# Block sums of the w_k gradient placed in other memory, and the sums at the start of the last stage put in another order

## The chip, the cores and the metric

One core of one Trainium2 chip runs the whole program in one launch. The metric is device time in microseconds (us), the median of several runs; lower is better. TensorE is called PE here, VectorE DVE, ScalarE ACT, GpSimd POOL, and SP is the queue from which most transfers are issued.

## The reference

The kernel computes one transformer block and all its gradients for one sequence of S = 2048 rows, D = 640, F = 1728, 32 heads of 20, all bf16:

```python
h  = x + A(layernorm(x))          # A: linear attention with wqkv, wo
h2 = h + B(layernorm(h))          # B: (silu(x @ w_gate) * (x @ w_up)) @ w_down
out, vjp = jax.vjp(f, A_x, A_wqkv, A_wo, B_w_gate, B_w_up, B_w_down)
return (out, *vjp(grad_out))
```

Three results matter for the change. `out_1` is the gradient of x; its last step is a layer norm backward over `dxn`, the gradient of the normalised input. `out_2` holds the gradient of wqkv; its middle third, the w_k gradient, is `xn.T @ dk`, a sum over 2048 rows. `out_0` is `h + m @ w_down`, where m is the product of the two gates.

## The kernel before

**Stages.** The program goes through the forward pass, the gate and up products with their gradients, and the attention gradients. Its last two stages are those that the change touches. The first is a loop (L1050 on) over t = 0 to 18. In step t it makes tile t of `dk` (128 rows; PE, then DVE L1057 to L1063), transposes it by DMA into the buffer `ring`, and for tile u = t - 3 makes `ps_dxn` on PE (L1095, 30 matmuls), and then the layer norm backward `ln_bwd` (L141 to L152): ACT scales the row (`lb_dy`, L144), DVE multiplies and sums (L146), scales two sums (L149), ACT makes `lb_a` (L150), DVE adds twice (L151, L152) into `dx`, and POOL issues the store of `dx` to `out_1` (L1103). In steps 16 to 18 there is no `dk` tile left, only `dxn` tiles 13, 14 and 15.

**The last stage** (from L1222) makes the w_k gradient and then `out_0`. Both are 2 x 2 block products in Winograd's form, which takes seven products in place of eight for the price of sums of blocks; DVE makes the sums with `tt` (L1033).

- For the w_k gradient the halves of the 2048 rows and the two halves of 640 columns are the blocks. Sums of blocks of xn are S1, S2, S3 (two of each, u = 0 and 1, 128 x 1024), sums of blocks of dk are X1 to X4 (128 x 2560, tile `dt`). S1 and S3 lie in the tile `sk`, and are made inside the loop above, at steps 16 to 18 (`ksum`). PE's products are `ps_ka` and `ps_kc` (L1162, by `prod`). The first products, of plain blocks, need no sum. The next, `ps_kc`, needs S1 and X1. Four small products `dwo` (L1110) stand between them. The last 128 rows of the gradient are outside the 2 x 2 scheme, and are made plainly, in three pieces of 320, 192 and 128 columns by `k_tile` (L1341) at the very end.
- For `out_0`, eight pairs p of row tiles go through `step_a` to `step_f` (PE: `ps_oa`, `ps_oc`). Sums of w_down's blocks are T1 to T5 (tile `ot`, T3 in place in `wd`), made once. Sums of m's blocks are four for each pair (`osum(p, 0)` to `osum(p, 3)`, in the tile `os`), of transposed tiles of m (`mT`, loaded by DMA, L1028). `step_d` and `step_e` of pair p - 1 stand between the steps of pair p.

**What sets the order.** PE, ACT, DVE and SP run in the order written here (`manual_schedule`); each engine does its instructions one after the other, and an instruction that waits holds up all those behind it. POOL's order is found by the framework. Work tiles come from pools with a fixed number of buffers; a new tile takes the place of an older one, and its first writer waits until all readers of that one are done, a store by DMA included. Four buffers of the pool `strips` and five of `big` are the places for the large tiles; four banks of PSUM are shared by all products (`mm`). The tiles of `ln_bwd` (`lb_dy`, `lb_a`, `dx`) come from a pool of six; before, all three of a row tile are taken together.

**Where the tiles lie before.** `mT` number 0 takes the place of the first `dq` tile, and `sk` that of the second, which SP still reads for the last transpose `ring<-dq` (L973). S2 lies in `os`; `os` has the place of `dh1`, which the last `dx` reads, and `dt` that of `wqkvT`, which the last `dxn` reads.

Of the kernel before, what the change touches and what calls it, by code (L numbers as in the profile page):

```python
# [20 lines left out]
def kernel(  # L21
# [40 lines left out]
    def mm(name):  # L62

        return psum.tile([P, 2, 512], FP32, name=name, tag="mm")
# [73 lines left out]
        eng.tensor_scalar(out=v[:, :nt], in0=mv[:, :nt, 1], scalar1=1e-5, scalar2=None, op0=ALU.add)  # L138
        nc.gpsimd.tensor_tensor(out=rstd[:, t0:t0 + nt], in0=v[:, :nt], in1=nhalf[:, :nt], op=ALU.pow)

    def ln_bwd(ps, xhat, rstd_col, resid, dst, pool):  # L141
        sums = small.tile([P, 2], FP32, name="lb_s", tag="lb_s")
        dy = wk("lb_dy", pool=pool)
        nc.scalar.activation(out=half(dy[:]), in_=row(ps), func=ACT.Copy, scale=rstd_col, accum_out=sums[:, 0:1])  # L144
        a = wk("lb_a", pool=pool)
        nc.vector.tensor_tensor_reduce(out=a[:], in0=dy[:], in1=xhat, scale=1.0, scalar=0.0,  # L146
                                       op0=ALU.mult, op1=ALU.add, accum_out=sums[:, 1:2])
        k = small.tile([P, 2], FP32, name="lb_k", tag="lb_k")
        nc.vector.tensor_scalar(out=k[:], in0=sums[:], scalar1=-1.0 / D, scalar2=None, op0=ALU.mult)  # L149
        nc.scalar.activation(out=a[:], in_=xhat, func=ACT.Identity, scale=k[:, 1:2], bias=k[:, 0:1])  # L150
        nc.vector.tensor_tensor(out=a[:], in0=a[:], in1=dy[:], op=ALU.add)  # L151
        nc.vector.tensor_tensor(out=dst, in0=a[:], in1=resid, op=ALU.add)  # L152

# [769 lines left out]
    with tc.manual_schedule(engines={EngineType.SP, EngineType.DVE}):  # L923
# [119 lines left out]
        def ksum(i, u):  # L1043

            if i == 1:
                tt(sk_v(1, u), xb(1, 0, u), xb(1, 1, u), ALU.add)
            else:
                tt(sk_v(3, u), xb(0, 0, u), xb(1, 0, u))

        for t in range(ST + LAG):  # L1050
            if t in (2, 3):
                dwqk(0, t + 1)
            if t < ST:
                if t + 2 < ST:
                    load_pk(t + 2)
                pkr = pkrs.pop(t)
                nc.vector.tensor_scalar(out=pkr[:], in0=pkr[:], scalar1=-1e-6, scalar2=1.0, op0=ALU.add, op1=ALU.min)  # L1057
                tk = wk("tk", pool=1)
                ps = mm("ps_dk")
                mm_row(ps, lambda i: xnT_r[:, t, i, :], lambda i, n0, n1: WK2[:, i, n0:n1], DT)  # L1060
                nc.vector.scalar_tensor_tensor(out=half(tk[:]), in0=row(ps), scalar=rstd1[:, t:t + 1] if t < NC else 1.0,
                                               in1=half(dzb[:]), op0=ALU.mult, op1=ALU.add)
                nc.vector.tensor_tensor(out=dk[:, t, :], in0=tk[:], in1=pkr[:], op=ALU.mult)  # L1063
                nc.sync.dma_start_transpose(out=ring[:, t % 4], in_=dk[:, t, :])
                if t < 2:
                    load_pqT(t + 1)
            if 8 <= t < 8 + HG:
                tr_cols(G[:, t - 8, :], scr_GT, OH[t - 8])
            if t == 14:
                nc.sync.dma_start_transpose(out=KV.rearrange("p j c -> p (j c)").unsqueeze(1), in_=scr_KVT)  # L1070
            if t == ST:
                dKV = stage()[:, :HG, :]
                nc.sync.dma_start_transpose(out=dKV, in_=dKVT.rearrange("p j c -> p (j c)"))
            if t == ST:
                wd = big.tile([P, FT, D], BF16, name="wd", tag="B")
                nc.sync.dma_start(out=wd[:, :13, :], in_=B_w_down[0:13 * P, :].rearrange("(j p) d -> p j d", p=P))
                for r in (0, 64):
                    nc.sync.dma_start(out=wd[r:r + 64, 13, :], in_=B_w_down[13 * P:F, :])
            u = t - LAG
            if u < 0:  # L1080
                continue
            if t == ST:
                sk = strips.tile([P, 7 * 8 * P], BF16, name="sk", tag="S")
                ksum(1, 0)
            if t == ST + 1:
                ksum(3, 0)
                ksum(3, 1)
            if t == ST + 2:
                ksum(1, 1)
            pkT, dqT, dkT = ring[:, 4 + u % 3], ring[:, 7 + u % 3], ring[:, u % 4]  # L1090
            ps = mm("ps_dxn")
            for ci, (n0, n1) in enumerate(NCH):
                for k, (lhs, rhs) in enumerate(((dqT, wqkvT[:, 0:5]), (pkT, WV2), (dkT, wqkvT[:, 5:10]))):
                    for i in range(DT):
                        nc.tensor.matmul(ps[:, ci, :320], lhsT=lhs[:, i, :], rhs=rhs[:, i, n0:n1],  # L1095
                                         start=(k == 0 and i == 0), stop=(k == 2 and i == DT - 1))
            if u + 3 < ST:
                load_pqT(u + 3)
            if ST - 4 <= u:
                load_mT(u - ST + 4)  # L1100
            dx = wk("dx")
            ln_bwd(ps, xn_r[:, u, :], rstd1[:, u:u + 1], dh1[:, u, :], dx[:], 0)
            nc.gpsimd.dma_start(out=o1_v[:, u, :], in_=dx[:])  # L1103

        def dwo(j):
            h0, h1 = HC[j]
# [19 lines left out]

        NP = ST // 2
        HK = 6
        os = big.tile([P, ST * D], BF16, name="os", tag="B")
        dt = big.tile([P, 4, 8, 320], BF16, name="dt", tag="B")  # L1130
        ot = strips.tile([P, 3 * HK * 320 + D], BF16, name="ot", tag="S")
        B11, B12 = wd[:, 0:HK, 0:320], wd[:, 0:HK, 320:D]
# [1 line left out]
        T1, T2, T4 = (ot[:, i * HK * 320:(i + 1) * HK * 320].rearrange("p (k n) -> p k n", k=HK) for i in range(3))  # L1134
        T3 = B12
        T5 = ot[:, 3 * HK * 320:3 * HK * 320 + D].rearrange("p (k n) -> p k n", k=2)
        f32 = os[:, 8 * HK * P:].bitcast(FP32)
        s1h, u3h, *u2h = (f32[:, 320 * i:320 * i + 320] for i in range(4))

        def os_v(p, i):  # L1140
            o = (4 * (p % 2) + i) * HK * P
            return os[:, o:o + HK * P].rearrange("p (k c) -> p k c", c=P)
# [81 lines left out]
        with tc.manual_schedule(engines={EngineType.PE, EngineType.Activation}):  # L1224
# [1 line left out]
            K21, K22 = dk[:, 8:16, 0:320], dk[:, 8:16, 320:D]  # L1226
            X1, X2, X3, X4 = (dt[:, i] for i in range(4))
            S1, S3 = [sk_v(1, u) for u in U], [sk_v(3, u) for u in U]
            S2 = [os[:, (3 + u) * 8 * P:(4 + u) * 8 * P].rearrange("p (k c) -> p k c", c=P) for u in U]
            kept = sk[:, 4 * 8 * P:4 * 8 * P + 4 * D].bitcast(FP32).rearrange("p (k u n) -> p k u n", k=2, u=2)  # L1230

            def k_store(ev, m, n):
# [4 lines left out]

            for t in range(4):
                load_h1(t)
            for t in range(4, 7):  # L1240
                load_mT(t)
            for j in range(2):
                tr_cols(Y[:, j, :], scr_Yt, OH[j])
            pk_a = [mm("ps_ka") for _ in U]
            for u in U:
                prod(pk_a[u][:, 0, :320], xb(0, 0, u), K11, True, 8)
            tt(X1, K12, K11)
            for u in U:
                prod(pk_a[u][:, 1, :320], xb(0, 1, u), K21, True, 8)
            for u in U:  # L1250
                tt(S2[u], S1[u], xb(0, 0, u))
            tt(X2, K22, X1)
            ev = wk("dwk", pool=1)
            for u in U:
                s1 = wk("s1", pool=u).bitcast(FP32)
                nc.scalar.copy(out=s1, in_=pk_a[u][:, 0, :320])
                tt(ev[:, 320 * u:320 * u + 320], pk_a[u][:, 1, :320], s1, ALU.add)
            k_store(ev, 0, 0)
            dwo(0)
            pk_c = mm("ps_kc")  # L1260
            for u in U:
# [10 lines left out]
            for u in U:  # L1272
                prod(pk_a[u][:, 0, :320], S3[u], X3, False, 8)
                nc.scalar.copy(out=kept[:, 1, u, :], in_=pk_a[u][:, 0, :320])
            for u in U:
                tt(S1[u], xb(0, 1, u), S2[u])
            dwo(3)
            ev = wk("dwk", pool=0)
            tt(half(ev[:]), pk_c[:, :, :320], kept[:, 1], ALU.add)
            k_store(ev, 1, 1)  # L1280
            tt(T2, B22, T1)
            osum(0, 1)
            ev = wk("dwk", pool=1)
            for u in U:
                prod(pk_a[u][:, 0, :320], xb(1, 1, u), X4, False, 8)
                nc.scalar.copy(out=ev[:, 320 * u:320 * u + 320], in_=pk_a[u][:, 0, :320])
            k_store(ev, 1, 0)

            def k_last(u):
                prod(pk_c[:, u, :320], S1[u], K22, False, 8)  # L1290

            for p in range(NP):
# [8 lines left out]
                    tr_cols(Y[:, j, :], scr_Yt, OH[j])  # L1301
                step_a(p)
                if v < 0:
                    tt(T4, B21, T2)
                    tt(T3, B22, B12)
                    osum(p, 2)
                    k_last(0)
                    pcc = mm("ps_oc")
                    step_b(p)
                    k_last(1)  # L1310
                    ev = wk("dwk", pool=0)
                    tt(half(ev[:]), pk_c[:, :, :320], kept[:, 0], ALU.add)
                    k_store(ev, 0, 1)
                    step_c(p)
                    tt(T5, BL[0], BL[1])
                    osum(p, 3)
                    for i in range(4):
                        osum(p + 1, i)
                    continue
                step_d(v)  # L1320
                step_b(p)
# [9 lines left out]
                f(i)  # L1331

            v = NP - 1
            i = DT - 1
            ev = wk("dwk", pool=1)
            pk_l = mm("ps_kl")
            last = [(pk_l[:, 0, :320], 0, 320), (pk_l[:, 1, :192], 320, 512)]

            def k_tile(out, n0, n1, queue):
                for t in range(ST):  # L1340
                    nc.tensor.matmul(out, lhsT=xn_r[:, t, i * P:(i + 1) * P], rhs=dk[:, t, n0:n1],  # L1341
                                     start=(t == 0), stop=(t == ST - 1))
                nc.scalar.copy(out=ev[:, n0:n1], in_=out)
                queue.dma_start(out=out_2[i * P:(i + 1) * P, D + n0:D + n1], in_=ev[:, n0:n1])

            k_tile(*last[0], nc.sync)
            step_d(v)
            k_tile(*last[1], nc.sync)
            c22(v)
            step_e(v)  # L1350
            step_f(v)
# [31 lines left out]
```

## Time and profile before

| | |
|---|---|
| median of 3 runs | 801.03 us (800.27 to 803.26) |
| the profiled execution, its own time | 801.46 us |
| its span, first to last instruction | 799.7 us |
| outside the span | 1.76 us |
| busy, share of the span | PE 99%, DVE 73%, ACT 36%, POOL 22% |
| PE waits from 660 us on | 4.0 us before `ps_kc`, 0.8 us before a `ps_oa` |
| last matmul starts its group | 795.3 us |

Times inside the execution are counted from the start of the span. Names before `<-` are what an instruction writes, names after it what it reads, and L1162 is line 1162 of the kernel before. In the chain of waits, a line is a start time, a length and the work that held up the end at that moment. In the list of waits, a line says who waited, for whom, how long in all, how often, and the longest. In the timeline, start and length come first, and the brackets at the end tell how long the engine was idle before it.

### The profile page before, as it was taken

To read this page: it belongs to the slowest core of one execution; us is meant where nothing else is said; L and a number is where in the kernel's file an instruction comes from. 1 tells how busy PE (TensorE), PEld (TensorE's weight loads), DVE (VectorE), ACT (ScalarE), POOL (GpSimd) and SP (SyncE) were. 2 spreads that over 40 slices of the span, in tenths; PEclk is the share of its full clock that TensorE was granted. 3 is DMA by queue.
4 is the path that set the end of the run, shared out by engine and by line. 5 is a ranking of instruction groups with operands and counts; after the bars stand their busy time and mean duration, and the time that the engine had idled before them with its cause. 6 is when DMAs were issued, how large, how long until landed. Compare 5 with 4: busy or idle time off the path is not lost.

```text
span 799.7 us, 13627 instructions
## 1 busy us (share of the span) xinstructions
PE 789.5 (99%) x5295; PEld 504.1 (63%) x5295; DVE 582.5 (73%) x1038; ACT 288.7 (36%) x420; POOL 174.0 (22%) x308
## 2 busy tenths in 40 slices
PE   9999999999999999999999999999999999979998
PEld 7776566555555555555666777777777777756665
DVE  7989988894496648844965169999896366658773
ACT  6963532760383146303821232232322233332001
POOL 4600047411201110012142011121401111214220
PEclk9999999999999999999999999999999999999999
DMA  9899999999979897991797567776599769999952
GB/s 258 168 242 309 186 233 248 276 217 230 195 178 223 211 181 196 224 233 59 169 256 193 210 171 197 180 206 166 146 236 188 141 142 180 173 262 264 224 168 75
DMA packets 286994, 160.11 MB, mean 200 GB/s; under 512 B 241629, under 2 KB 275806, under 8 KB 286929
## 3 DMA queue, kind: packets, MB, share of 16 engines
q1 hardware_dynamic: 269056, 99.74, 61.6%
q0 software_dynamic: 14976, 54.20, 21.7%
q10 hardware_dynamic: 2896, 5.31, 2.1%
q8 instruction: 41, 0.67, 0.4%
q14 instruction: 25, 0.20, 0.1%
HBM read 47.68 MB, written 53.66 MB: 127 GB/s over the span
## 4 chain that ended last, share of the span: by engine, by line
PE 88%; DVE 5%; DMA 5%; ACT 0%; POOL 0%; SPq 0%; issue 0%; DVEq 0%
PE ps_dhn L108 15%; PE ps_dw L806 8%; PE ps_dxn L1095 7%; PE ps_wa L646 7%; PE pg L731 6%; PE pu L736 6%; PE ps_dm L417 5%; PE ps_oa L1162 4%; PE ps_kq L305 4%; PE ps_wc L646 3%; PE ps_dwqk L986 3%; PE ps_gt L861 3%; PE ps_dk L108 3%; PE ps_dp L108 3%; PE ps_y L508 3%; PE ps_a L571 3%
## 5 line engine op out<-in xcount | busy, mean ns | idle before, releaser
L108 PE MATMUL ps_dhn<-wgT,cols 128*128 128x320 bf16 x864 | 119.5, 299 | 0.0
L108 PEld LDWEIGHTS <-cols 128*128 128x128 bf16 x864 | 84.5, 98 | 32.9
L736 PE MATMUL pu<-wgu,hnT 128*128 128x448 bf16 (+1 forms) x320 | 63.6, 346 | 0.0
L731 PE MATMUL pg<-wgu,hnT 128*128 128x448 bf16 (+1 forms) x320 | 63.6, 346 | 0.0
L806 PE MATMUL ps_dw<-m_s,dh 128*128 128x448 bf16 (+1 forms) x320 | 60.4, 346 | 0.0
L1095 PEld LDWEIGHTS <-ring 128*128 128x128 bf16 x480 | 46.8, 98 | 18.8 <-DMA ring<-dq 0.7
L146 DVE CUSTOM_DVE_ANT_0 lb_a<-lb_dy,hn 128x640 bf16<-128x640 bf16 x32 | 26.4, 825 | 42.9 <-ACT lb_dy L144 42.9
L1095 PE MATMUL ps_dxn<-wqkvT,ring 128*128 128x320 bf16 x320 | 51.2, 299 | 0.0
L806 PEld LDWEIGHTS <-dh 128*128 128x128 bf16 x320 | 31.3, 98 | 27.1
L736 PEld LDWEIGHTS <-hnT 128*128 128x128 bf16 x320 | 31.3, 98 | 27.1
L731 PEld LDWEIGHTS <-hnT 128*128 128x128 bf16 x320 | 31.3, 98 | 27.0
L417 PEld LDWEIGHTS <-dh2T 128*128 128x128 bf16 x320 | 31.0, 98 | 25.1
L417 PE MATMUL ps_dm<-wdT,dh2T 128*128 128x448 bf16 (+1 forms) x240 | 46.5, 344 | 0.0
L144 ACT ACTIVATE lb_dy<-ps_dhn,rstd 128x640 bf16<-128x640 f32 x16 | 12.7, 794 | 91.7 <-PE ps_dhn L108 91.7
L305 PE MATMUL ps_kq<-wqk,xnT 128*128 128x320 bf16 x320 | 44.8, 299 | 0.2 <-DMA xnT<-xn 0.2
L752 ACT ACTIVATE dd<-pg 128x896 bf16<-128x896 f32 (+1 forms) x32 | 28.5, 891 | 40.4 <-PE pg L731 38.0
L642 DVE TENSOR_TENSOR dd<-dd 128x3584 bf16<-128x3584 bf16 (+1 forms) x12 | 23.1, 1954 | 25.3 <-PE ps_wa L646 15.6
L150 ACT ACTIVATE lb_a<-hn,lb_k 128x640 bf16<-128x640 bf16 x32 | 29.4, 920 | 27.8 <-DVE lb_k L149 24.8
L305 PEld LDWEIGHTS <-xnT 128*128 128x128 bf16 x320 | 30.9, 98 | 12.7 <-DMA xnT<-xn 0.5
L646 PEld LDWEIGHTS <-S 128*128 128x128 bf16 x256 | 25.0, 98 | 22.1 <-DVE dd L642 0.6
L772 POOL DMA_DIRECT2D scr_m<-m_s x16 | 12.1, 756 | 122.6 <-DVE m_s L764 122.6
L885 POOL DMA_DIRECT2D pqr<-scr_pq x16 | 8.8, 548 | 112.6 <-PE ps_dp L108 112.6
(227 smaller groups left out, 1566.5 us busy)
## 6 DMA issues: line engine op xcount, KB each, us to landing
scr_dT<-stg SPq DMA_DIRECT2D x48, 224.0 KB, 2.7
cols<-scr_dT POOLq DMA_DIRECT2D x6, 1728.0 KB, 9.0
scr_m<-m_s POOLq DMA_DIRECT2D x12, 448.0 KB, 4.8
cols<-scr_dT ACTq DMA_DIRECT2D x2, 1728.0 KB, 11.4
scr_dT<-stg SPq DMA_DIRECT2D x16, 192.0 KB, 2.3
scr_pq<-pqa SPq DMA_DIRECT2D x4, 640.0 KB, 4.6
scr_xnT<-xnT SPq DMA_DIRECT2D x4, 640.0 KB, 5.2
scr_pk<-pk SPq DMA_DIRECT2D x4, 640.0 KB, 4.6
```

Source lines behind the costliest of these rows:

```text
L108: nc.tensor.matmul(ps[:, ci, :320], lhsT=lhs(k), rhs=rhs(k, *NCH[ci]), start=(start and k == 0), stop=(stop and k == n - 1))
L146: nc.vector.tensor_tensor_reduce(out=a[:], in0=dy[:], in1=xhat, scale=1.0, scalar=0.0, op0=ALU.mult, op1=ALU.add, accum_out=sums[:, 1:2])
L150: nc.scalar.activation(out=a[:], in_=xhat, func=ACT.Identity, scale=k[:, 1:2], bias=k[:, 0:1])
L305: nc.tensor.matmul(ps[:, ci, :320], lhsT=xnT[:, t, k, :], rhs=wqk[:, k, w0 + n0:w0 + n1], start=(k == 0), stop=(k == DT - 1))
L417: nc.tensor.matmul(ps[:, c, :w], lhsT=dh2T[:, kt, (t + c) * P:(t + c + 1) * P], rhs=wdT[:, kt, o:o + w], start=(kt == 0), stop=(kt == DT - 1))
L646: nc.tensor.matmul(out, lhsT=lhs[:, t, :], rhs=rhs[:, t, :], start=(first and t == 0), stop=(t == 7), skip_group_check=not first)
L731: nc.tensor.matmul(pg[:, c, :w], lhsT=hnT[:, kt, (t + c) * P:(t + c + 1) * P], rhs=wg[:, kt, 0:w], start=(kt == 0), stop=(kt == DT - 1))
L736: nc.tensor.matmul(pu[:, c, :w], lhsT=hnT[:, kt, (t + c) * P:(t + c + 1) * P], rhs=wg[:, kt, w:2 * w], start=(kt == 0), stop=(kt == DT - 1))
L752: sig = nc.scalar.activation(out=dg, in_=pg[:, :, :w], func=ACT.Sigmoid)
L806: nc.tensor.matmul(ps[:, c, :w], lhsT=lhs(t), rhs=rhs(t), start=(t == 0), stop=(t == ST - 1))
L1095: nc.tensor.matmul(ps[:, ci, :320], lhsT=lhs[:, i, :], rhs=rhs[:, i, n0:n1], start=(k == 0 and i == 0), stop=(k == 2 and i == DT - 1))
L1162: nc.tensor.matmul(out, lhsT=lhs[:, k, :], rhs=rhs[:, k, :], start=(start and k == 0), stop=(k == n - 1), skip_group_check=not start)
```

## The change

1. `sk` is taken at step 15, ahead of `mT` number 0, so it has the place of the first `dq` tile, and `mT` number 0 that of the second. The sums S1 are both made at step 16 and the sums S3 both at step 17. The loads of `mT` begin one step later: the first is issued after the load of w_down (`wd`).
2. `ln_bwd` becomes a generator `ln_bwd_parts`, which pauses after ACT's `lb_a`. For the last row tile (u = 15) its first part runs after the order for X1, and its second part (`dx_end`) after the first eviction of the w_k gradient; so its tiles `lb_dy` and `lb_a` are taken after the four `h1r` buffers.
3. X1 is made ahead of that layer norm. S2 lies in `ot`; `os` is taken after `dx_end`.
4. T4, T5 and the sums for the first pairs are put in another order; the update of S1 (`xb(0, 1, u) - S2`) is made after an eviction in place of before it.
5. The 320-column piece of `k_tile` moves from ahead of the last `step_d` to pair 0, after `step_c`; its store goes to POOL's queue in place of SP's, and its evicted tile (`k_ev`) is taken there and held to the end.

```diff
-    def ln_bwd(ps, xhat, rstd_col, resid, dst, pool):
+    def ln_bwd(*args):
+        for _ in ln_bwd_parts(*args):
+            pass
+
+    def ln_bwd_parts(ps, xhat, rstd_col, resid, dst, pool):
...
         nc.scalar.activation(out=a[:], in_=xhat, func=ACT.Identity, scale=k[:, 1:2], bias=k[:, 0:1])
+        yield
         nc.vector.tensor_tensor(out=a[:], in0=a[:], in1=dy[:], op=ALU.add)
         nc.vector.tensor_tensor(out=dst, in0=a[:], in1=resid, op=ALU.add)
...
-            if t == ST:
+            if t == ST - 1:
                 sk = strips.tile([P, 7 * 8 * P], BF16, name="sk", tag="S")
-                ksum(1, 0)
-            if t == ST + 1:
-                ksum(3, 0)
-                ksum(3, 1)
-            if t == ST + 2:
-                ksum(1, 1)
+            if t in (ST, ST + 1):
+                for n in U:
+                    ksum((1, 3)[t - ST], n)
...
-            if ST - 4 <= u:
-                load_mT(u - ST + 4)
+            if ST - 3 <= u:
+                load_mT(u - ST + 3)
             dx = wk("dx")
-            ln_bwd(ps, xn_r[:, u, :], rstd1[:, u:u + 1], dh1[:, u, :], dx[:], 0)
+            ln = ln_bwd_parts(ps, xn_r[:, u, :], rstd1[:, u:u + 1], dh1[:, u, :], dx[:], 0)
+            if u == ST - 1:
+                break
+            for _ in ln:
+                pass
             nc.gpsimd.dma_start(out=o1_v[:, u, :], in_=dx[:])
+
+        def dx_end():
+            for _ in ln:
+                pass
+            nc.gpsimd.dma_start(out=o1_v[:, ST - 1, :], in_=dx[:])
...
-            S2 = [os[:, (3 + u) * 8 * P:(4 + u) * 8 * P].rearrange("p (k c) -> p k c", c=P) for u in U]
+            S2 = [ot[:, 2 * HK * 320 + u * 8 * P:2 * HK * 320 + (u + 1) * 8 * P].rearrange("p (k c) -> p k c", c=P)
+                  for u in U]
...
-            for t in range(4, 7):
+            for t in range(3, 7):
                 load_mT(t)
...
             for u in U:
                 prod(pk_a[u][:, 0, :320], xb(0, 0, u), K11, True, 8)
+            for u in U:
+                prod(pk_a[u][:, 1, :320], xb(0, 1, u), K21, True, 8)
             tt(X1, K12, K11)
-            for u in U:
-                prod(pk_a[u][:, 1, :320], xb(0, 1, u), K21, True, 8)
+            next(ln)
             for u in U:
                 tt(S2[u], S1[u], xb(0, 0, u))
             tt(X2, K22, X1)
...
             k_store(ev, 0, 0)
+            dx_end()
+            os = big.tile([P, ST * D], BF16, name="os", tag="B")
...
-            for u in U:
-                tt(S1[u], xb(0, 1, u), S2[u])
-            dwo(3)
             ev = wk("dwk", pool=0)
             tt(half(ev[:]), pk_c[:, :, :320], kept[:, 1], ALU.add)
             k_store(ev, 1, 1)
+            dwo(3)
+            for u in U:
+                tt(S1[u], xb(0, 1, u), S2[u])
...
                 step_a(p)
                 if v < 0:
-                    tt(T4, B21, T2)
                     tt(T3, B22, B12)
...
                     step_c(p)
+                    tt(T4, B21, T2)
+                    k_tile(mm("ps_kl")[:, 0, :320], 0, 320, nc.gpsimd)
+                    osum(p + 1, 0)
+                    osum(p + 1, 1)
                     tt(T5, BL[0], BL[1])
                     osum(p, 3)
-                    for i in range(4):
-                        osum(p + 1, i)
+                    osum(p + 1, 2)
+                    osum(p + 1, 3)
                     continue
...
-            k_tile(*last[0], nc.sync)
             step_d(v)
-            k_tile(*last[1], nc.sync)
+            k_tile(mm("ps_kl")[:, 0, :192], 320, 512, nc.sync)
             c22(v)
```

## The prediction on record

> **What bounds the kernel now.** The page's first part comes first: PE is busy 99% of the span, so only time that PE stands still, or runs at a lower clock, can be won; the change takes no matmul away. Whether there is such time in the last two stages, the list of waits of 690 to 800 us tells.
>
> ```profile
> PE ps_kc L1162 <- DVE dt L1033: 4.0, 1, 4.0
> ...
> ACT s L1256 <- DMA out_dram<-dx: 2.2, 1, 2.2
> ...
> PE ps_oa L1162 <- DVE h1r L1033: 0.8, 1, 0.8
> ```
>
> PE waits twice. Why the first wait is there, the chain of waits shows, read from the top:
>
> ```profile
> 702.48 3.97 DMA ring<-dq
> 706.53 0.69 DVE sk L1033
> 707.22 0.74 DVE lb_a L146
> ...
> 717.83 1.50 DVE dt L1033
> 719.37 3.18 PE ps_kc L1162 x16
> 722.56 0.53 PE ps_dwo L1110 x2
> 723.09 2.75 PE ps_ka L1162 x16
> 725.84 0.27 PE ps_dwo L1110 x2
> 726.11 2.17 PE ps_ka L1162 x16
> ```
>
> DVE stands still from 702.2 to 706.5: `sk` lies where the last transpose still reads `dq`. Three layer norms queue up behind it, and X1 (`dt`) behind them. The same lines hold a second loss: sixteen matmuls take 3.18 and 2.75 us after the wait and 2.17 at 726; two take 0.53 and then 0.27. The windows confirm it, granted clock third from the end:
>
> ```profile
> 715.00:720.00 5.00, 0.98 (x8) 0.50 (x7) 3.91 (x8) 1.87 (x4) 1.76 (x4) 1.00 1.21 277
> 720.00:725.00 5.00, 5.00 (x27) 3.07 (x25) 5.00 (x6) 1.30 (x3) 2.17 (x4) 0.66 1.22 261
> 725.00:730.00 5.00, 5.00 (x39) 3.62 (x37) 4.48 (x7) 3.00 (x7) 1.44 (x3) 1.00 1.20 323
> ```
>
> The second wait (741.36) has DVE behind it too: from 733.7 to 741.2 it worked without a pause on sums.
>
> [...] 4.0 us idle, then 0.66 granted over 5 us. [...] POOL's store of `dx` took 2.4 us from issue to landing when issued at 702.49, and 6.9 at 710.46, while the 2 MB of `wd` moved (issued at 707.01, 9.8 to landing).
>
> **The change part by part.** Clock as before up to 702.1, where DVE ends the `dx` of u = 12.
>
> *Sums in earlier memory.* The first `dq` tile was read for the last time many steps ago, so DVE needn't wait. Pitches from DVE's timeline: a 1024-wide sum 0.60, a whole layer norm from L146 to the end of L152 2.95 (707.14 to 710.09, ACT's turn included), a 2560-wide sum 1.40. Then: S1 to 703.3; layer norm 13 to 706.3; S3 to 707.5; layer norm 14 to 710.4; X1 must wait for the last `dxn` matmul (its place was `wqkvT`'s), which ends at 710.6, so it is done at 712.1, against 719.3 before. PE needs it when `ps_ka` (to 714.92) and `dwo(0)` (0.27) are through, at 715.2: 3.1 to spare. The wait goes: 4.01. With it goes the half clock: (3.18 - 2.17) + (0.53 - 0.27) + (2.75 - 2.17) = 1.85.
>
> *Split layer norm, and its new wait.* Taken after the four `h1r` buffers, `lb_dy` of u = 15 no longer gets an old `lb_dy` but the buffer of `dx` 13, whose store must land before ACT may write. The page of before has this kind of wait: ACT's `s` above waited 2.2 us for a store of `dx`. Now `dx` 13 is done at 706.3, and POOL issues its store 0.3 later (710.17 to 710.46 before), at 706.6. `wd` is issued 1.6 earlier than before, as no `mT` load (1.58 of SP) is ahead of it: at 705.4. [...] I take the 6.9 us seen in that position: landing at 713.5. Lower end 2.4, landing at 709.0; upper end: it drains with `wd` as before's did (710.46 + 6.87 = 717.33), 1.6 earlier, at 715.7. Queued behind that wait are, on ACT, `lb_a`, the two `s` and the copy of `dwo(0)`; on DVE all after X1. What must be met: L146 starts 1.0 after the landing (`lb_dy` 0.9); then L146 to L149 1.0, S2 1.2, X2 1.4, evictions 0.8, the split layer norm's end 0.94, X3 1.4: X3 is there 7.8 after the landing. PE wants it after `ps_kc` 2.17, `dwo` 0.27, `ps_ka` 2.17 and `dwo` 0.27, at 715.2 + 4.9 = 720.1. So PE loses (landing - 712.3): 1.2 at 713.5, nothing at 709.0, 3.4 at 715.7. The other needs (S2 and X2 at 717.6, the bank of `ps_kc` at 715.2) are met later than that value allows, so they add nothing. The store of `dx` 14, which `dx` 15 needs, is queued with the same load, but is wanted only some 6 us after.
>
> *Other memory for S2 and `os`.* `ot` lies where `ring` lay, whose last transpose landed at 706.5; S2 comes at 713: nothing. `os` waits for the split layer norm's end, and its first use is the sum after T1, seven DVE steps later: nothing.
>
> *`mT` behind `wd`.* In sum the queue carries the same bytes. The second `mT` tile took 10.0 from 709.74, so it landed at 719.7; it keeps that place, and the first now comes shortly before it. DVE wants the second at 721.3 or later, PE the first at 724.7: nothing, with 1.6 of cover. Lost cover would cost PE its lateness one for one.
>
> *Order of T4, T5 and the sums.* T4 (1.07) and two sums pass each other, the amount is the same. DVE is now ahead of PE here, because `k_tile` (2.18) gives it time: from the end of `step_c` it has an eviction 0.5, T4, five sums and T5, 3.9, and two evictions 0.9, in all 5.5 with a step between engines; PE has 2.17 for `k_tile` and 4.05 (736.48 to 740.53 before) until `step_c` of pair 1, 6.2. So the wait of 0.84 goes, with 0.7 to spare.
>
> *Moved chunk.* The same 16 matmuls in another place: nothing on PE. At the end, `step_d` of the last pair now follows `dwv` at once. It needs the eviction of `step_c`, which DVE ended at 786.3, and `dwv` ended at 788.3: covered by 2.0. Its store is one POOL issue of 0.54 behind an ACT copy, ahead of an `h1r` load wanted 20 us later; SP loses one issue. `k_ev` holds one of seven buffers for the stage; loads of `h1r` led their use by over 10 us, and a buffer comes free each 7.25: covered.
>
> *Sum.* 4.01 + 1.85 + 0.84 - 1.2 = 5.5 us. The profiled execution, 801.46, would take 796.0 (span 799.7 to 794.2). The median of the runs is 0.43 below that execution; the gain taken off it: 801.03 - 5.5 = 795.5.
>
> **The rivals.**
>
> *A: the store isn't in the way.* `dx` 13 gets into the engines before `wd`, or between its packets. For it: `dx` 12 took 2.4 among transposes. Against: `wd` has a lead of 1.2 us. Gain 6.7: 794.3.
>
> *B: the store drains with `wd`.* For it: before's store landed at 717.3, just past `wd`'s 716.8. Against: it was issued late in that transfer, so the two ends had to be near. Loss 3.4, gain 3.3: 797.7.
>
> *C: slower than before, by the same wait.* If the store lands behind `wd` and the first `mT` load that now follows it, [...] the clock is halved again, 1.85. The change gains nothing once (landing - 712.3) + 1.85 exceeds 6.7, from a landing at 717.2 on; at 718.5 it is 6.2 + 1.85 = 8.1, a loss of 1.4: 802.4. For it: stores issued at 714.6, among `mT` loads, still took 4.4. Against: its own bytes are few, and `wd` starts earlier.
>
> *That the change does nothing* would need X1 to be late in another way; it has 3.1 us of cover, so I give it no chance of its own.
>
> **How the numbers follow.** Forecast 0.45, A 0.22, B 0.25, C 0.08. I predict 795.5; forecast and A together span 794.3 to 796.5 (a landing at 714.5). For 8 in 10 the range takes in A and B: down to 793.8 for 0.5 of scatter, up to 799.2, B with most of a half clock on top. About 0.5% (4.0 us) is what a measurement of this kernel can tell from no change. Faster by more than that, below 797.0: forecast, A and a little of B, 0.68. Within it: most of B, and C near its start, 0.28. Slower: 0.04.
>
> **What the profile would show.** Right: no wait of PE for `dt` and none for `h1r`; clock 1.00 from 715 to 730; DVE's `sk` straight after `dx` at 702; a wait of ACT's `lb_dy` for a store of `dx`, ending near 713.5; then a wait of PE of about 1 us in all before `ps_ka` or a `dwo`. Under A no such waits; under B about 3 us of them; under C a clock below 1. What would make it wrong: a landing other than that, or an `mT` tile later than 721.

## The result: 2 us of the 5.5 forecast

The changed kernel takes 799.18 us in the median of 20 runs (795.3 to 806.74), the kernel before 802.01 in 20 runs beside it (799.86 to 805.17): 0.9972 of the time before, 95% interval 0.9950 to 0.9994. The gain is about 2 us where 5.5 were forecast. In all, 56 runs of the changed kernel were made; their median is 800.0 us, against 801.97 in 221 runs of the kernel before. The profiled execution took 798.42 us, span 796.7; the last group of matmuls starts at 792.81 instead of 795.16 (by PE's timeline; the 795.3 in the table of before is the chain's reading of the same group).

The list of waits of the kernel after, 690 to 800 us (who waited, line, for whom; total, times, longest):

```profile
ACT lb_dy L148 <- DMA out_dram<-dx: 3.9, 1, 3.9
...
PE ps_dwo L1121 <- ACT dwo L1122: 2.1, 1, 2.1
...
PE ps_dwv L127 <- DMA mats<-scr_Yt: 1.7, 1, 1.7
...
PE ps_dxn L1097 <- DMA ring<-dq: 0.6, 1, 0.6
```

The waits of before for `dt` (4.0) and for `h1r` (0.8) are gone. Three others stand in their place, 4.4 us together against 4.85. The windows view (granted clock third from the end) says that in this execution the half clock went too:

```profile
715.00:720.00 5.00, 2.95 (x22) 1.99 (x21) 4.83 (x9) 2.25 (x4) 0.50 (x1) 1.00 1.00 168
720.00:725.00 5.00, 4.96 (x37) 3.59 (x37) 4.83 (x5) 2.56 (x5) 2.74 (x6) 1.00 1.13 266
```

The chain of waits of the kernel after (start, length, what held up the end):

```profile
704.95 11.13 DMA wd<-in_B_w_down_dram
...
719.29 0.70 ACT dwo L1122
719.99 0.04 issue
720.03 0.43 PE ps_dwo L1121 x2
720.47 2.17 PE ps_ka L1169 x16
...
753.60 5.31 DMA mats<-scr_Yt
758.91 0.05 issue
758.95 0.19 PE ps_dwv L127
```

Where before DVE's `sk`, `lb_a` and `dt` stood, the chain now runs through transfers: first `wd`, then the transposes of `Yt`, which `ps_dwv` reads. The first link needs care. The instruction behind it on DVE (S2) waits for several things, and the view names one; DVE's `lb_k` had ended at 715.97, just before S2 began at 716.11, so it was the late layer norm that held S2. (In `a3` below S2 starts 0.14 us after `lb_k` too, at 715.57, before `wd` has landed at 715.77.) ACT's, PE's and DVE's timelines show what follows:

```profile
714.02 0.79 ACT L148 ACTIVATE lb_dy<-ps_dxn,rstd 128x640 bf16<-128x640 f32 x1 [3.93 <-DMA out_dram<-dx]
...
719.29 0.69 ACT L1122 CAST dwo<-ps_dwo 128x640 bf16<-128x640 f32 x1 [1.67 <-DVE dwk L1038]
```

```profile
715.61 2.34 PE L1169 MATMUL ps_kc<-dt,sk 128*128 128x320 bf16 x16
720.03 0.43 PE L1121 MATMUL ps_dwo<-mats 128*128 128x320 bf16 x2 [2.09 <-ACT dwo L1122]
```

```profile
711.19 1.49 DVE L1038 TENSOR_TENSOR dt<-dk 128x2560 bf16<-128x2560 bf16 x1
```

X1 (`dt`) is ready at 712.7, as forecast; then ACT stands for the store of `dx` 13, which lands at 713.9, and so its copy of the first `dwo`, which the second `dwo` waits for, ends at 720.0. Why the `Yt` loads come late, SP's timeline shows. Before:

```profile
709.74 17.55 SPq L1028 DMA_TRANSPOSE mT<-scr_m  x6
727.33 2.60 SPq L938 DMA_TRANSPOSE mats<-scr_Yt  x2
...
745.46 2.59 SPq L938 DMA_TRANSPOSE mats<-scr_Yt  x2
```

After:

```profile
707.11 27.06 SPq L1033 DMA_TRANSPOSE mT<-scr_m  x7
734.21 3.15 SPq L943 DMA_TRANSPOSE mats<-scr_Yt  x2
...
752.28 2.58 SPq L943 DMA_TRANSPOSE mats<-scr_Yt  x2
```

Seven `mT` loads stand behind `wd` where six stood, and the first and the last pair of `Yt` loads are issued 7 us later, the pair between them 3 us. One more load explains only 2 to 3 us of the 7: the loads behind the first of each row also left SP 3.1 us apart, where it was 2.2 before, and what slowed them is not shown. The load that moved has a later landing of its own. The DMA view of the instant it is issued in, before and after (us from issue to landing last):

```profile
mT<-scr_m SPq DMA_TRANSPOSE x1, 4.3
```

```profile
mT<-scr_m SPq DMA_TRANSPOSE x1, 13.5
```

Ahead of `wd`, its issue kept SP for 1.6 us and it landed 4.3 us after it. Behind `wd`, the issue alone kept SP from 707.1 to 715.7, the 2 MB of `wd` landed at 716.1, and all other loads of the queue stood behind that.

### The profile page after: what moved, and what is told of

It is laid out like the page before. It is cut to its first block, busy times and chain, and to the rows that moved or that the text cites. A ratio compares the mean times of both kernels' runs of the same rounds, so it can differ in the third digit from the quotient of the medians.

```text
span 796.7 us, 13634 instructions
## 1 busy us (share of the span) xinstructions
PE 787.8 (99%) x5295; PEld 504.1 (63%) x5295; DVE 583.2 (73%) x1038; ACT 288.9 (36%) x420; POOL 174.3 (22%) x309
## 4 chain that ended last, share of the span: by engine, by line
PE 90%; SPq 4%; DMA 3%; DVE 2%; issue 0%; POOL 0%; ACT 0%; DVEq 0%; ACTq 0%
PE ps_dhn L108 15%; PE ps_dw L811 10%; PE ps_wa L651 7%; PE pu L741 7%; PE pg L736 7%; PE ps_dxn L1097 7%; PE ps_dm L422 5%; PE ps_kq L310 4%; PE ps_wc L651 3%; PE ps_dwqk L991 3%; PE ps_gt L866 3%; PE ps_dp L108 3%; PE ps_y L513 3%; PE ps_dk L108 3%; PE ps_a L576 3%; SPq L1033 2%
```

## The experiments

**Theory:** the freed time is lost again to two waits, the store of `dx` 13 (2.1 us at `ps_dwo`) and the transfers behind `wd` (`mT`, then `Yt`), and to half-clock windows that such waits bring. **Rival:** the clock, or DMA traffic in general, takes it whatever is done about the two.

One sum holds all profiles together. From the start of the last `dk` tile on PE to the start of the last matmul group it takes 95.8 us, plus PE's waits in the list, plus 1.7 us for each window of 3.4 us at half clock. Before: 795.16 - 692.54 = 102.62 = 96.07 + 4.85 + 1.7. After: 792.81 - 692.54 = 100.27 = 95.87 + 4.4. In all seventeen profiles the rest lies between 95.0 and 96.3, though the last two columns of this table vary widely:

| kernel | median us (runs) | to before, 95% interval | profile: PE's waits, us | half-clock windows |
|---|---|---|---|---|
| before (first profile / `b2`) | 801.7 (10, `b2`) | 1.0000 (0.9985-1.0015) | 4.85 / 4.2 | 1 / 1 |
| after (first / `a2` / `a3`) | 799.2 / 800.8 / 800.3 (20/22/14) | 0.9972 (0.9950-0.9994) / 0.9981 (0.9966-0.9996) / 0.9982 (0.9958-1.0005) | 4.4 / 3.1 / 5.0 | 0 / 1 / 1 |
| `e1_lndy_in_ot` | 801.2 (22) | 0.9986 (0.9969-1.0003) | 4.9 | 1 |
| `e2_yt_early` | 799.2 (10) | 0.9968 (0.9952-0.9984) | 2.0 | 1 |
| `e3_both` | 798.7 (6) | 0.9954 (0.9939-0.9968) | 3.1 | 0 |
| `e4_sums_only` | 801.2 (14) | 0.9990 (0.9974-1.0005) | 5.2 | 1 |
| `e5_mt_ahead` / `e11` (again) | 795.0 / 796.4 (5/7) | 0.9926 (0.9910-0.9941) / 0.9935 (0.9912-0.9958) | 0.6 / 1.9 | 0 / 0 |
| `e6_chunk_back` | 800.3 (22) | 0.9993 (0.9978-1.0008) | 4.1 | 0 |
| `e7_mt_ahead_only` | 798.6 (22) | 0.9962 (0.9949-0.9976) | 2.7 | 1 |
| `e8_two_more_mt_b` | 805.1 (22) | 1.0025 (1.0009-1.0041) | 8.2 | 2 |
| `e9_h1r_late` | 802.4 (22) | 1.0000 (0.9985-1.0016) | 3.5 | 1 |
| `e10_mt_ahead_h1r_late` / `e12` (again) | 801.3 / 800.1 (14/19) | 0.9993 (0.9975-1.0012) / 0.9974 (0.9958-0.9990) | 0.4 / 5.9 | 0 / 2 |

(The half-clock windows at the very end, which begin after the last matmul group has begun, are not counted. `e9`'s profile has one more wait, at 193 us, and a window behind it, far from the stage that was edited.)

**The changed kernel again (`a2`, `a3`).** 

> The changed kernel again, nothing edited, so that the other runs of this batch have it beside them on the same chip. Theory: PE loses 2.1 us at the second ps_dwo (the lb_dy of the last row tile waits for the store of dx 13) and 1.7 us at ps_dwv (the Yt transposes land late); 799 us, 2 to 3 us under the kernel before.

> The changed kernel a third time, beside e11_mt_ahead_again. Theory: 799 to 801 us, PE idle 3 to 4.5 us behind the dxn loop, none to two half-clock windows. Rival for e11_mt_ahead_again's gain (this chip is merely quick): 796 us here too.

The store's wait is in both (2.5 and 1.8 us). `Yt` is waited for in `a3` (2.7 us) and not in `a2`. Part of that is that `a2` came late itself: its last `Yt` load landed at 757.5 instead of 758.9, but its half-clock window brought PE to `ps_dwv` only at 758.6, instead of 756.8. `a3`'s list of waits and windows read:

```profile
PE ps_dwv L127 <- DMA mats<-scr_Yt: 2.7, 2, 2.5
PE ps_dwo L1121 <- ACT dwo L1122: 1.8, 1, 1.8
```

```profile
760.00:765.00 5.00, 5.00 (x27) 2.67 (x26) 1.47 (x3) 0.51 (x1) 1.17 (x3) 0.67 1.16 230
```

So the same program loses here what it did not lose there: the transfers land at somewhat different times in each execution, and they have no cover left.

**The last layer norm without the store's wait (`e1`).**

```diff
-        dy = wk("lb_dy", pool=pool)
+        dy = pool()[0] if callable(pool) else wk("lb_dy", pool=pool)
...
-        a = wk("lb_a", pool=pool)
+        a = pool()[1] if callable(pool) else wk("lb_a", pool=pool)
...
-            ln = ln_bwd_parts(ps, xn_r[:, u, :], rstd1[:, u:u + 1], dh1[:, u, :], dx[:], 0)
+            ln = ln_bwd_parts(ps, xn_r[:, u, :], rstd1[:, u:u + 1], dh1[:, u, :], dx[:],
+                              0 if u < ST - 1 else lambda: (ot[:, 0:D], ot[:, D:2 * D]))
```

> The two work tiles of the last layer norm lie in free columns of ot, so it waits for no store. Theory (two waits one behind the other): the ps_dwo wait of 2.1 us goes, PE reaches ps_dwv 2.1 us sooner, the Yt transposes land no sooner (758.9 on the trace's clock), and their wait grows from 1.7 to about 3.8 us: no gain, 799 us, perhaps worse through a half-clock window behind so long a wait. Rival (the store wait alone is what the forecast missed by too little): the whole 2.1 us is won, 797 us.

801.2 us beside `a2`'s 800.8. No wait at `ps_dwo` is left, and nothing is gained, as the theory has it; the wait for `Yt` is 2.8 instead of 1.7 us. It did not reach 3.8, because PE came 2.1 us late into the stage by a wait for `ring<-dq` (below).

**`Yt` early (`e2`), and both (`e3`).**

```diff
+            if 2 <= t < 2 + HG:
+                tr_cols(Y[:, t - 2, :], scr_Yt, OH[t - 2])
             if 8 <= t < 8 + HG:
                 tr_cols(G[:, t - 8, :], scr_GT, OH[t - 8])
...
-            for j in range(2):
-                tr_cols(Y[:, j, :], scr_Yt, OH[j])
...
-                for j in range(2 * p + 2, min(2 * p + 4, HG)):
-                    tr_cols(Y[:, j, :], scr_Yt, OH[j])
```

> The six Yt transposes are taken in the dxn loop (t = 2 to 7), not behind the mT loads. Theory: no wait at ps_dwv, the ps_dwo wait stays at 2.1 us: 1.7 us faster than the changed kernel, 797.5 us. Rival (the missing gain is in the clock or in DMA contention in general): the time stays at 799 us, another transfer is late in place of Yt.

> Both edits at once: no wait for the store of dx 13 and Yt transposed early. Theory: both waits gone, 2.1 + 1.7 = 3.8 us faster than the changed kernel, 795.4 us, and no half-clock window behind the waits, so that the runs scatter less. Rival (clock or contention): 799 us with the same scatter.

`e2` takes 799.2 us, 1.6 under `a2` on the same chip, near the 1.7 that its theory names, though the two intervals overlap. The wait for `Yt` is gone; its profile has neither of the two waits, but one of 2.0 us for `ring<-dq`, so it cannot price the store. `e3` gains 2 us on `a2` and not 3.8. The theory was too narrow: with both named waits gone, the next transfer in the same queue is late. PE's wait in `e3`'s list, and DVE's timeline:

```profile
PE ps_kc L1172 <- DVE sk L1038: 1.7, 1, 1.7
```

```profile
727.12 0.56 DVE L1038 TENSOR_TENSOR os<-mT 128x768 bf16<-128x768 bf16 x1 [5.24 <-DMA mT<-scr_m]
```

DVE stands 5.24 us for the second `mT` tile, and the sums for `ps_kc` are queued behind that. It is the whole queue behind `wd`, not the `Yt` loads in particular.

**`mT` ahead of `wd` (`e5`, again as `e11`).** As `e1`, with

```diff
-            if 8 <= t < 8 + HG:
-                tr_cols(G[:, t - 8, :], scr_GT, OH[t - 8])
+            if 2 <= t < 2 + HG:
+                tr_cols(G[:, t - 2, :], scr_GT, OH[t - 2])
+            if 9 <= t < 13:
+                load_mT(t - 9)
...
-            if t in (ST, ST + 1):
-                for n in U:
-                    ksum((1, 3)[t - ST], n)
...
-            if ST - 3 <= u:
-                load_mT(u - ST + 3)
...
+            if u == ST - 2:
+                for n in U:
+                    ksum(1, n)
...
-            for t in range(3, 7):
+            for t in range(4, 7):
                 load_mT(t)
...
             tt(X3, K22, K12)
+            for n in U:
+                ksum(3, n)
```

So the first `dq` tile holds `mT` number 0 and the second holds `sk`; the sums S1 come after the layer norm of u = 14, the sums S3 after X3.

> The changed kernel with its last layer norm in ot and with the first four mT loads ahead of wd: they go into the first dq tile during the dxn loop (t = 9 to 12, the G loads move to t = 2 to 7 for them), sk goes into the second and its sums behind the layer norms. Yt loads stay where they are. Theory (the queue behind wd is the limit): some 9 us less stand in the queue behind wd, mT and Yt land ahead of need, PE waits nowhere for 0.5 us after the dxn loop: 793 to 795 us, 4 to 6 us under the changed kernel. Rival (the losses are jitter of the clock and of the dq transposes): 798 us or more, like the other edits.

> e5_mt_ahead once more, since its time rests on five runs: the same kernel beside the changed kernel on one chip. Theory (PE's idle time behind the dxn loop is the loss, and this kernel has next to none): 795 to 796 us, at least 4 us under the changed kernel. Rival (its five runs were a lucky draw of the half-clock windows): 798 us or more, with the windows of the changed kernel.

795.0 and, on another chip beside `a3`'s 800.3, 796.4 us. It is the fastest version. All that PE waits for from 620 us on in `e5`:

```profile
PE ps_ka L1170 <- DVE sk L1038: 0.4, 1, 0.4
PE ps_dxn L1096 <- DMA ring<-dq: 0.2, 1, 0.2
```

None of its twelve runs shows a half-clock window in its mean clock (0.999 or 1.0 in all), while 38 of the 56 of the changed kernel do (0.998 or less). The ratios to before, 0.9926 and 0.9935, are gains of 5.2 to 5.9 us: the forecast's 5.5 were there to be had. (The edit also moves the `G` loads and DVE's sums. That these bring a gain of their own is not tested; the list of waits leaves them no more than the 0.4 us for `sk`.)

**The same with the store's wait (`e7`).** As `e5`, with `lb_dy` and `lb_a` in their old pool.

> The changed kernel with the first four mT loads ahead of wd (with the moves that this needs, as in e5_mt_ahead), the last layer norm in its own buffers again, so that it waits for the store of dx 13. Theory (two losses, the queue and the store): the queue's waits go, the wait for the store stays and costs PE 2 us once, some of it with a half-clock window: 796 to 798 us, 1 to 3 above e5_mt_ahead's 795.0. Rival (the store is the whole loss and mT ahead only covers): 799 us; other rival (the store never mattered): 795 us.

798.6 us, a little over the theory's band (796 to 798), and by the number alone as near to the first rival's 799. What speaks against that rival is `e1`, where the store's wait went and nothing was won. The whole list of PE's waits from 620 us on is one line, and it brings a half-clock window (0.66 granted from 720 to 725):

```profile
PE ps_dwo L1121 <- ACT dwo L1122: 2.7, 1, 2.7
```

With that, one chip has all four combinations: both waits in the way 800.3 and 800.8 us (`a3`, `a2`), the store's removed 801.2 (`e1`), the queue's removed 798.6 (`e7`), both removed 796.4 (`e11`). The store's wait costs 2.2 us where the queue is out of the way and nothing that shows where it is not; neither alone is the loss.

**More loads in the queue (`e8`).** Two of the `mT` loads behind `wd` are taken twice.

```diff
-            for t in range(3, 7):
+            for t in (3, 4, 5, 6, 3, 5):
                 load_mT(t)
```

> The changed kernel with two mT loads behind wd taken twice (rows 3 and 5 again behind row 6, the same bytes to the same place), nothing else. Theory (the queue behind wd sets when Yt lands): the first Yt transposes are issued two mT loads, 4 to 5 us, later, the last land as much later, and PE's waits grow by that: 803 to 805 us. Rival (Yt is late by chance and the queue has slack): 799 to 801 us.

805.1 us, 4 to 6 above the changed kernel. The size is the theory's, but by luck. PE meets no wait for `Yt`; it meets DVE's wait for `mT`, with two half-clock windows behind it:

```profile
DVE os L1038 <- DMA mT<-scr_m: 7.3, 1, 7.3
...
PE ps_oc L1169 <- DVE os L1038: 4.3, 1, 4.3
```

```profile
741.80 0.56 DVE L1038 TENSOR_TENSOR os<-mT 128x768 bf16<-128x768 bf16 x1 [7.35 <-DMA mT<-scr_m]
```

This sum reads `mT` tile 3 (`osum(1, 0)`), which the edit writes a second time. The tile was first there at 727.3; the repeated load was issued at 733.8 and landed at 741.78, just ahead of DVE's start. So the edit itself made DVE wait for the repeated tile, and the time of `e8` says nothing on what a longer queue costs PE. What it does show is that two more loads put off the issue of the first `Yt` load, to 739.2 from 734.2.

**One part of the change alone (`e4`).** The kernel before with

```diff
-            if t == ST:
+            if t == ST - 1:
                 sk = strips.tile([P, 7 * 8 * P], BF16, name="sk", tag="S")
-                ksum(1, 0)
...
+            if t in (ST, ST + 1):
+                for n in U:
+                    ksum((1, 3)[t - ST], n)
```

and `mT` behind `wd`. 

> The kernel before with one part of the change: sk is taken one step sooner, so that it lies where the first dq tile was, and the four sums stand ahead of their layer norms; its mT loads come behind wd, as in the changed kernel. Layer norm not split, S2 in os, order of T4 and T5 and the chunk as before. Theory (the DMA queue behind wd takes back what DVE gains): the 4.0 us wait for X1 goes; the last layer norm uses buffers that wait for no store, so no wait for dx 13; but the mT and Yt loads come as late as in the changed kernel and PE stands still for them, 1.7 us or more: 798 to 800 us. Rival (the split and the place of S2 are what brings the gain): a wait of PE of 1.5 us or more for X1 or X3 stays, 801 us.

The rival's time came, 801.2 us, but not the wait of 1.5 us or more for X1 or X3 that it named: X1, still behind the whole last layer norm, costs 0.9 us, and 3.3 are lost at `ps_dwo`:

```profile
PE ps_dwo L1107 <- ACT dwo L1108: 3.3, 1, 3.3
```

ACT's copy `s` ahead of it waits for a store of `dx` there, as in the kernel before, and that wait now ends at 721.0, behind `wd`. So a store is in the way with either order; the theory's claim that this layout has none was false. The new place of the sums alone brings nothing that can be told from no change (0.9990 of before).

**The moved chunk undone (`e6`).** 

> The changed kernel with the 320-column chunk of the last w_k tile back at the end. Theory (Yt is bound by the queue): PE reaches ps_dwv 2.2 us sooner, Yt lands no sooner, so its wait grows from 1.7 or less to 2.2 to 3.9 us, and at pair 1 a wait of about 0.8 us for h1r returns: 2 to 3 us slower than the changed kernel, 801 to 802 us. Rival (a moved chunk costs and brings nothing, as the prediction has it beyond the 0.84): 0.8 us slower, 800 us.

800.3 us, the rival's figure, not the theory's; but it ran on another chip than `a2`, and its ratio to before (0.9993) and those of the changed kernel (0.9972 to 0.9982) have overlapping intervals, so this prices little. The profile shows the forecast part: the wait for `h1r` is back, 1.6 us. The wait for `Yt` is 0.2, not 2.2 or more; the transposes were issued 3 us sooner than in the first profile of after (749.1 against 752.3), and PE was late by 2.3 for `ring<-dq`.

**The kernel before again (`b2`).** 

> The kernel before again, for a second profile of it. Theory: PE waits 4 us for dt and 0.8 us for h1r, one half-clock window or two behind the first, 801 to 802 us. What it tells apart: the wait of 0.6 to 2.3 us for ring<-dq in the profiles of the changed kernel and its edits. If it comes with the change, it is absent here again; if it is chance, it can be here too.

```profile
PE ps_dxn L1095 <- DMA ring<-dq: 2.1, 1, 2.1
PE ps_kc L1162 <- DVE dt L1033: 0.9, 1, 0.9
PE ps_oa L1162 <- DVE h1r L1033: 0.8, 1, 0.8
PE ps_ka L1162 <- DVE dwk L1033: 0.4, 1, 0.4
```

The wait for `ring<-dq` is here too, though not in the first profile of before: it comes without the change. And the 4.0 us for X1 that the forecast took off are not a fixed sum: where PE is late already, 0.9 is left of them. Total 4.2 against 4.85. The kernel before absorbs this delay in its own wait; the changed one, with no such wait left, pays it in full.

**`h1r` late (`e9`, `e10`, `e12`).** The first four loads of `h1r` are ordered behind the store of `dx` 14 (`e10` and `e12`: in `e5`).

> The changed kernel with its first four h1r loads behind the store of dx 14 in POOL's order (two stood among the dq transposes at 697 to 698 us, a third beside the store of dx 13). Theory (the ring<-dq wait at 702 us comes from a dq transpose issued together with these loads): no wait of PE there, dq lands within 4 us, the other waits stay: about 1 us faster, 798 us, less scatter. Rival (dq lands late whatever stands beside it): 799 to 800 us with the same scatter and again a wait of 0.6 to 2 us in the profile.

> e5_mt_ahead with its first four h1r loads behind the store of dx 14. Theory: nothing of PE's idle time after 695 us is left but the 0.4 us before ps_ka: 794.5 to 795 us, the same as e5_mt_ahead within its scatter. Rival (h1r, now landing later, is missed by the first pairs): 796 us or more, with a wait for h1r near 727 us.

> e10_mt_ahead_h1r_late once more on the same chip, for a second profile: its first profile (795.3 us) is not like most of its runs (801 us). Theory (h1r loads issued together behind the dx stores and wd come late in most executions): a wait of PE or DVE for h1r or mT of 2 us or more in the profile, 801 us. Rival (the other chip, or an early wait unrelated to the edit): 795 us here.

In all three profiles the wait for `ring<-dq` is gone, as the theory has it, but the time is not better. `e9` takes 802.4 us, of which this stage is not the cause: after the wait at 193 us its last `dk` tile starts at 696.5 instead of 692.5, and from there to the last matmul group it takes 101.1 us, where the three profiles of the changed kernel take 100.3 to 102.6. `e10` and `e12` take 801.3 and 800.1 us, 4.8 and 3.7 above `e11` (796.4, same chip as `e12`). The profile of `e10` is of its fastest run of 14, 795.3 us, with 0.4 of waits; that of `e12` is of its slowest of 19, 803.8 us, and shows what such a run meets:

```profile
PE ps_dwv L127 <- DMA mats<-scr_Yt: 4.2, 2, 3.3
```

Four loads of 160 KB put behind `wd` undo what four `mT` loads ahead of it had won. They are in POOL's queue and not in SP's, and SP's transfers are later all the same: its first `mT` load behind `wd` landed 18.0 us after its issue, against 9.2 in `e11`, and its first `Yt` load was issued at 730.8, against 721.0. So the order of SP's queue is not all here: with those four loads in POOL's queue SP's own landed later.

## Why the prediction was wrong, step by step

- *Sums in earlier memory: the 4.01 us go.* Right in the mechanism, and in the times: X1 at 712.7 for 712.1. As a size it holds for the first profile of before only (in `b2` 0.9 are left of it, behind a wait of 2.1).
- *The half clock: 1.85 go.* Failed in most executions. It went from where it was, but windows came back behind the new waits (`a2` near 721, `a3` at 760). Mean clocks of 0.998 or less are in 38 of 56 runs after; before, in 167 of the 201 whose clock is on record.
- *Split layer norm and its wait.* The landing was right, 713.9 for 713.5; the loss was not, 2.1 (1.8 and 2.5 in `a3` and `a2`) for 1.2. The step took X3, wanted at 720.1, for the first need. The need that comes first is the second `dwo`'s, at 717.95: all four PSUM buffers (`mm`) are in use, so it waits for ACT's copy of the first `dwo`, which stands behind the two `s` and the DVE evictions, at 720.0. The prediction named that copy as queued and did not ask when PE wants it. The second `dwo` started 6.1 us after the landing; wanted at 715.2 + 2.2 = 717.4 on the prediction's clock, it costs (landing - 711.3), which at the forecast landing is 2.2. The landing came 7.3 us after the issue. By the DMA records of after, the first data packet of POOL's queue moved 4.2 us after the store's issue (706.66 to 710.82), where `wd`'s first had moved 1.1 us after its own (704.95 to 706.07); in before the store beside `wd` shows the same, 4.1 us (710.46 to 714.52) of its 6.9. What held it up is not shown.
- *"mT behind wd: nothing, with 1.6 of cover".* **The step that failed.** It argued that the queue carries the same bytes and that the second `mT` tile keeps 719.7. The two tiles landed at 720.6 and 722.6, which cost PE nothing in this profile. But the walk along SP's queue ended with `mT`: the `Yt` loads behind it, the last pair 7 us later, are in no line of the prediction. The last of them landed at 758.9, and PE wanted it at 757.3: 1.7 us. In `a3` it was 2.7, and in `e3`, with `Yt` out of the queue, 1.7 at the second `mT` tile. The profiles agree on the queue: with three `mT` loads behind `wd` the first `Yt` load is issued at 721.0 to 723.5 (`e5`, `e7`, `e11`), with six at 727.3 and 727.5 (before, `b2`), with seven at 730.2 to 734.4 (after, `a2`, `a3`, `e1`, `e4`, `e6`), with nine at 739.2 (`e8`); `e9` is left out for its late start, `e10` and `e12` for their moved `h1r` loads. `e5` and `e11` show that PE gets the time back when the row is short.
- *Other memory for S2 and `os`: nothing.* Right: S2 began 0.1 us after the layer norm's `lb_k`.
- *Order of T4, T5: 0.84.* Right: no wait for `h1r` in the three profiles of the changed kernel, and it is back in `e6`, where `k_tile` gives DVE no time.
- *Moved chunk: nothing.* Not shown by itself: `e6` undoes it, but is too near to the others to price it.
- *Sum.* 4.01 + 0.84 + 1.85 - 1.2 should read, for the profiled execution, 6.7 - 2.1 - 1.7 - 0.6 = 2.3; the starts of the last matmul groups differ by 2.35. The 0.6 is the wait for `ring<-dq`; the rest of the span's 3.0 is its end, 0.7 shorter after the last matmul. The runs without a half-clock window (mean clock above 0.998) have medians of 800.4 before and 797.9 after, those with one 802.2 and 802.5.

Rival B came nearest by its time (797.7), but not by its cause: the store did not drain with `wd`; it landed 2.2 us ahead of it.

**What stays open.** Why PE waits 2.0 to 2.3 us for a transpose of `dq` in some executions (`b2`, `e1`, `e2`, `e6`) and 0 to 1.5 in others (0 in the first of before, 0.6 in that of after, 1.5 in `e11`); `h1r` loads stand beside it, and with them moved away (`e9`, `e10`, `e12`) the wait was never there, but three profiles are few. And what made seven `mT` loads behind `wd` leave SP more slowly than six.

## What to carry to other kernels

A transfer put later in SP's queue put off those behind it here (with seven `mT` loads behind `wd` in place of six, the first `Yt` load was issued at 734.2 us instead of 727.3), and it was paid for where one of them was wanted first (1.7 us at `ps_dwv`): walk the queue to its end, with landing times from the profile, and not to the transfer that was moved. In this stage a load of 2 MB took 9.8 us in before and 11.1 in after and `e5`, a store of 160 KB beside it 6.9 (before) instead of 2.4, and a transposing load behind it 13.5 (after) instead of 4.3 (before, ahead of it); the version that put four such loads ahead of it was the fastest. And where one wait covers another, take the waits off the profile one after the other: the 4.0 us of one profile of before were 0.9 in the next.

## What the runs showed that was not expected

PE's half clock came behind shorter waits than the 4.0 us of before, the only wait with a half clock behind it that the forecast had measured; that rival C would bring another was its estimate. Six lone waits of 1.4 to 1.8 us (after, `a3`, `e3`, `e6`, `e9`, `e11`) left the clock whole; waits of 1.9 to 2.3 us brought a window of 3.4 us in three cases (`b2`, `e2`, the early one of `e9`) and none in four (after, `e1`, `e6`, `e8`); all seven of 2.45 us or more did. Two waits close to each other, neither above 1.9 us, were followed by a window too: 1.22 and 0.61 us in `e9`, 1.88 and 0.90 in `e1`.

The clock records in the traces tell the middle cases apart. In all profiles, each half clock among the matmuls starts a whole number of times 3.413 us after the first full clock of the execution (210 times in the first profile of before, from 3.92 to 720.72, where 3.413 us at 0.50 begin; 205 in `b2`). Divide each execution into pieces of 3.413 us from that moment, and add up PE's idle time in each piece. Of the twelve pieces at full clock that a half clock follows, eleven have 1.99 to 3.41 us of idle time and one 1.82 (`e9`); no other piece up to the last matmul group has more than 1.95. So the 2.10 us in `b2` lie in one piece and bring the half clock, while the 2.09 at `ps_dwo` in the first profile of after are divided into 0.54 and 1.55 and do not; of the 4.01 us in before, 1.95 lie in one piece and 2.06 in the next. In these traces some 2 us of idle time in one piece came ahead of a half clock (2.06 of 3.41 in before).

So the wait of 2.09 us cost 2.1 us in the first profile of after, and that of 2.10 in `b2`, with the 1.7 of its window, 3.8: they differ in where they fall. That may be a part of why the runs of the changed kernel scatter over 11 us, and those of `e5` and `e11`, with little to wait for, over 5.4 (in 12 runs).
